# Sketched attention and an expert layer on one core: nine tiles moved into the routing, look-ahead and zero products at the start

## The chip, the core and the metric

One core of one Trainium2 chip runs the kernel. Its five engines are named here as the profile names them: PE (TensorE matmul; PEld is its weight load), DVE (VectorE), ACT (ScalarE), POOL (GpSimd) and SP (SyncE, which here only issues DMAs). Each works through its own list of instructions in order; semaphores tie the lists together. The metric is device time in microseconds (us) of one execution; lower is better.

## The reference

```python
# attention, per batch and head: r = 8, head_dim 32, 4 x 4 x 1088 positions
phi(x) = outer(S1 @ x, S2 @ x)                  # 64 numbers per position
kv, z = sum_s phi(k) v^T, sum_s phi(k)
x = phi(q) kv / (phi(q) z + 1e-6)               # N = 4352 tokens of 4 * 32 = 128 numbers
# experts: E = 8, F = 1024
logits = x @ w_gate
e = argmax(logits)                              # one expert per token
c = softmax(logits)[e] * sigmoid(x @ w_output_gate)[e]
out = c * (relu(x @ w1[e]) @ w2[e])
```

Everything is fp32. Which expert a token goes to is known only after its attention is done.

## The kernel before

The 4352 tokens are 34 chunks of 128, in nine groups of four (the last of two).

*Attention* runs as a software pipeline of steps (the loop at L456). A step may take a group of keys and a group of queries. `sketch` (L285) multiplies by S1 and S2 on PE (`ps_ab`), ACT copies half of the result out, `product` (L299) forms the outer products on DVE (`kp`, `qp`). `sums` (L332) adds keys times values into `ps_kvz` per batch; once a batch is complete, `close`, `gates_T` and `gates` make its right-hand side `kz`. A query group is transposed (`turned`, `ps_qT`), multiplied by `kz` (`attend`, `ps_nd`), and one step later divided and given its logits on DVE (`shared`, L370). The first three steps have keys alone, the last three queries alone; there are 12 steps and three more turns of the loop.

*Routing* goes by duos of groups (8, 8, 8, 4 and 6 chunks). `choose` (L391) takes the argmax and running counts per expert on DVE; in the next turn `place` (L421) turns them into positions on PE (`ps_pos`, in the PSUM buffer with the tag `rt`), and `send` (L428) makes the row numbers on DVE and lets POOL scatter the tokens' rows, one indirect DMA per chunk (L444), into a DRAM table `xs`. There each expert owns a stretch of CAP rows.

*Tables.* After the loop the counts come out of one more matmul (`ps_n`, L490), POOL scatters rows of padding behind each expert's tokens (L502), and some 20 DVE instructions (L492 to L540) make two tables for 41 tiles of 128 rows: the expert of each tile (`eti`) and its first row in `xs` (`bti`).

*Tiles.* For each tile SP reads a table entry and fetches 128 rows (`rows`, L549), and the two halves of the expert's weights (`weights`, L554, 512 KB each) into one of three buffers, unless that buffer already holds this expert; all three are filled with expert 0 at the start. On PE: `turn` (transpose, `ps_xs`), `up` (8 products, `ps_h`), then ReLU on ACT for even tiles and on DVE for odd ones, `down` (8 products, `ps_y`, which lies in the `kvz` buffer for even tiles and in `rt` for odd ones). ACT scales the result, POOL scatters it to the output (L585). A product in fp32 shows as two matmul rows in the trace. The order is written out by hand (L591 to L612): while tile t goes down, tile t+1 goes up and t+2 is turned; rows are fetched five tiles ahead, weights three.

Nothing of the tiles stands before the last of the routing, on any engine:

```python
for t in range(NX):
    rows(t)                 # reads xs: waits for every scatter, the padding's too
```

Of the kernel before, what the change touches and what calls it, by code (L numbers as in the profile page):

```python
# [12 lines left out]
F32 = mybir.dt.float32  # L13
# [6 lines left out]
GRP = 512  # L20
TS = 128
NW = 3
# [9 lines left out]
def kernel(  # L32
# [159 lines left out]
    RG = max(len(rs) for rs in routes)  # L192
    eps = consts.tile([128, 1], F32, tag="eps")
# [29 lines left out]

    KN = -(-N // TS)
    step_i = consts.tile([128, max(NT, KN)], I32, tag="step_i")
    nc.gpsimd.iota(step_i, pattern=[[1, max(NT, KN)]], base=0, channel_multiplier=0)
    step = consts.tile([128, max(NT, KN)], F32, tag="step")
    nc.gpsimd.tensor_copy(step, step_i)
    stepT = consts.tile([128, max(NT, KN)], F32, tag="stepT")
    nc.gpsimd.tensor_scalar_mul(stepT, step, float(TS))  # L230
    upto = consts.tile([128, E, E], F32, tag="upto")
    nc.gpsimd.memset(upto, 0.0)
    for e in range(E):
        nc.gpsimd.memset(upto[:, e, :e + 1], 1.0)
# [193 lines left out]
    def send(i, oh, cum, ey, pp):  # L428
# [14 lines left out]
        for j in range(n):  # L443
            apart("rows", nc.gpsimd.indirect_dma_start(  # L444
                out=xs[:, :], out_offset=bass.IndirectOffsetOnAxis(ap=sloti[:, j:j + 1], axis=0),
                in_=x[:, j], in_offset=None, bounds_check=E * CAP - 1))

    def sketches(step):  # L450
        return [None if g is None else (groups[g],) + sketch(src, groups[g]) for src, g in zip((kT, qT), step)]

    with tc.manual_schedule():
        made = sketches(steps[0])
        chosen = placed = late = None
        for n in range(len(steps) + 3):  # L456
# [3 lines left out]
            ended, fills = [], None  # L460
# [188 lines left out]
```

## Time and profile before

| | us |
|---|---|
| median of three runs | 269.72 (268.0 to 269.8) |
| the profiled execution | 269.85 |
| its span, first to last instruction | 268.1 |
| PE busy in the span | 215.1 (80%) |
| POOL busy in the span | 82.7 (31%) |
| mean granted PE clock | 0.929 of full |

The profile is one execution. Its granted clock is a share of 2.4 GHz: 1.00 is that level and 0.50 is 1.2 GHz. Busy shares are means over stages with different limits; what matters is what each stage waits for. Times in the rows below are from the span's start.

### The profile page before, as it was taken

To read this page: it belongs to the slowest core of one execution; us is meant where nothing else is said; L and a number is where in the kernel's file an instruction comes from. 1 tells how busy PE (TensorE), PEld (TensorE's weight loads), DVE (VectorE), ACT (ScalarE), POOL (GpSimd) and SP (SyncE) were. 2 spreads that over 40 slices of the span, in tenths; PEclk is the share of its full clock that TensorE was granted. 3 is DMA by queue.
4 is the path that set the end of the run, shared out by engine and by line. 5 is a ranking of instruction groups with operands and counts; after the bars stand their busy time and mean duration, and the time that the engine had idled before them with its cause. 6 is when DMAs were issued, how large, how long until landed. Compare 5 with 4: busy or idle time off the path is not lost.

```text
span 268.1 us, 6840 instructions
## 1 busy us (share of the span) xinstructions
PE 215.1 (80%) x2573; PEld 208.1 (78%) x2573; DVE 95.2 (36%) x237; ACT 58.8 (22%) x127; POOL 82.7 (31%) x135
## 2 busy tenths in 40 slices
PE   1759998999630002999999999999999999999960
PEld 1758897988530001999999999999999999999960
DVE  5134677788989000221222222222212222222200
ACT  1001423243420000122222221222222222212220
POOL 8000000575678760022212222212222122222140
PEclk9999999999965555799999999999999999999996
DMA  5999300011111112138568687887813777811000
GB/s 172 360 401 391 158 5 4 24 62 33 50 40 51 48 70 70 34 117 265 192 170 292 202 276 234 251 257 232 285 45 108 252 235 223 286 44 33 9 0 0
DMA packets 19456, 40.09 MB, mean 150 GB/s; under 512 B 3338, under 2 KB 8972, under 8 KB 19424
## 3 DMA queue, kind: packets, MB, share of 16 engines
q1 hardware_dynamic: 16880, 34.63, 39.4%
q0 software_dynamic: 2544, 5.03, 5.3%
q8 instruction: 20, 0.33, 0.5%
q14 instruction: 12, 0.10, 0.1%
HBM read 55.60 MB, written 5.48 MB: 228 GB/s over the span
## 4 chain that ended last, share of the span: by engine, by line
issue 46%; POOL 19%; DMA 2%; POOLq 2%; DVE 1%; DVEq 0%
POOL out_dram L585 14%; POOL xs L444 4%; DMA xs<-pad,pai 1%; POOLq L585 1%; DMA xin<-xs 1%; POOLq L645 0%; DVE x L379 0%; DVE L L385 0%; POOL x L441 0%; POOL x L442 0%; DVE lg L383 0%; DVE mx L400 0%; DVE sloti L435 0%; POOLq L444 0%; DVE co L440 0%
## 5 line engine op out<-in xcount | busy, mean ns | idle before, releaser
L572 PE MATMUL ps_h<-xsT,wt 128*128 128x128 f32 x656 | 81.7, 279 | 0.0
L582 PE MATMUL ps_y<-wt,hT 128*128 128x128 f32 x656 | 79.8, 275 | 0.0
L572 PEld LDWEIGHTS ps_h<-xsT,wt 128*128 128x128 f32 x656 | 78.3, 196 | 0.0
L585 POOL DMA_INDIRECT out_dram<-y,xin x41 | 39.8, 970 | 121.7 <-ACT y L584 119.0
L582 PEld LDWEIGHTS ps_y<-wt,hT 128*128 128x128 f32 x656 | 76.5, 192 | 0.0
L565 DVE COPY xsT<-ps_xs 128x128 f32<-128x128 f32 x41 | 12.0, 292 | 99.9 <-PE ps_xs L563 99.9
L444 POOL DMA_INDIRECT xs<-x,sloti x34 | 33.7, 993 | 11.2 <-issue 8.5
L576 DVE TENSOR_SCALAR hT<-ps_h 128x1024 f32<-128x1024 f32 x20 | 24.5, 1225 | 29.9 <-PE ps_h L572 29.9
L574 ACT ACTIVATE hT<-ps_h 128x1024 f32<-128x1024 f32 x21 | 21.5, 1024 | 61.6 <-PE ps_h L572 61.6
L584 ACT ACTIVATE y<-ps_y,xin 128x128 f32<-128x128 f32 x41 | 15.1, 368 | 81.3 <-PE ps_y L582 81.3
L563 PE MATMUL ps_xs<-ident,xin 128*128 128x128 f32 x41 | 11.7, 286 | 25.0 <-DMA xin<-xs 25.0
L563 PEld LDWEIGHTS ps_xs<-ident,xin 128*128 128x128 f32 x41 | 6.0, 147 | 25.3 <-DMA xin<-xs 25.3
L341 PE MATMUL ps_kvz<-vt,kp 128*64 128x65 f32 (+1 forms) x288 | 13.1, 246 | 6.3 <-DVE kp L304 6.3
L341 PEld LDWEIGHTS ps_kvz<-vt,kp 128*64 128x64 f32 (+1 forms) x288 | 11.2, 156 | 7.7 <-DVE kp L304 7.2
L304 DVE TENSOR_TENSOR kp<-ps_ab,b_sb 128x1024 f32<-128x1024 f32 (+1 forms) x9 | 10.4, 1157 | 16.3 <-ACT b_sb L296 16.3
L442 POOL TENSOR_TENSOR x<-co,ey 128x8 f32<-128x8 f32 (+2 forms) x5 | 1.4, 275 | 44.1 <-DVE co L440 44.1
L364 PE MATMUL ps_nd<-kz,qpT 128*64 128x98 f32 x272 | 13.4, 250 | 1.2 <-ACT qpT L356 1.2
L364 PEld LDWEIGHTS ps_nd<-kz,qpT 128*64 128x64 f32 x272 | 11.8, 136 | 2.3 <-ACT qpT L356 1.7
L292 PE MATMUL ps_ab<-Sb,kT 128*64 128x64 f32 x272 | 12.1, 254 | 0.5 <-DVE Sb L269 0.5
L292 PEld LDWEIGHTS ps_ab<-Sb,kT 128*64 128x64 f32 x272 | 10.9, 167 | 1.5 <-issue 0.8
L356 ACT COPY qpT<-ps_qT 128x1024 f32<-128x1024 f32 (+1 forms) x9 | 8.7, 965 | 15.4 <-PE ps_qT L354 15.4
L354 PE MATMUL ps_qT<-ident,qp 128*128 128x128 f32 x68 | 9.4, 279 | 1.9 <-DVE qp L304 1.9
(121 smaller groups left out, 123.4 us busy)
## 6 DMA issues: line engine op xcount, KB each, us to landing
wt<-in_w_dram SPq DMA_DIRECT2D x88, 512.0 KB
xin<-xs SPq DMA_DIRECT2D x41, 65.0 KB
vt<-in_v_dram SPq DMA_DIRECT2D x8, 260.0 KB
kT<-in_k_dram SPq DMA_DIRECT2D x8, 256.0 KB
qT<-in_q_dram SPq DMA_DIRECT2D x8, 256.0 KB
out_dram<-y,xin POOLq DMA_INDIRECT x41, 3.8
xs<-x,sloti POOLq DMA_INDIRECT x34, 2.3
vt<-in_v_dram SPq DMA_DIRECT2D x1, 130.0 KB
```

The costliest lines, as they stand in the source:

```text
L292: nc.tensor.matmul(ps[64 * t:64 * (t + 1), j * H:(j + 1) * H], src[:, c * 128 + 64 * t:c * 128 + 64 * (t + 1)], Sb[:, i], start=i == 0, st ...
L341: nc.tensor.matmul(acc[b][64 * h:64 * (h + 1), s], kp[p0:p0 + np_, j * H + 2 * s + h].rearrange("s i j -> s (i j)"), vt[p0:p0 + np_, c, s] ...
L364: nc.tensor.matmul(ps[64 * t:64 * (t + 1), 2 * j + s, :VG], qpT[:, 2 * j + s, 64 * t:64 * (t + 1)], kz[(c * 128 + 64 * t) // S][:, s], sta ...
L444: apart("rows", nc.gpsimd.indirect_dma_start(out=xs[:, :], out_offset=bass.IndirectOffsetOnAxis(ap=sloti[:, j:j + 1], axis=0), in_=x[:, j] ...
L563: nc.tensor.transpose(ps, xin[t][:, :DM], ident)
L565: nc.vector.tensor_copy(xTs[t], ps)
L572: nc.tensor.matmul(ps[:, c], wt[t % NW][0][:, c], xT, start=True, stop=True)
L574: nc.scalar.activation(hTs[t], ps, ACTF.Relu)
L576: nc.vector.tensor_scalar_max(hTs[t], ps, 0.0)
L582: nc.tensor.matmul(ps, hT[:, c], wt[t % NW][1][:, c], start=(c == 0), stop=(c == FC - 1))
L584: nc.scalar.activation(y, ps, ACTF.Copy, scale=x[:, DM:DM + 1])
L585: apart("out", nc.gpsimd.indirect_dma_start(out=out, out_offset=bass.IndirectOffsetOnAxis(ap=x.bitcast(I32)[:, DM + 1:DM + 2], axis=0), in ...
```

## The change

Four edits.

1. *Early tiles.* After the second duo (MARK = 1) 16 chunks have been routed. Whatever their experts, 2048 tokens fill at least NE = 9 tiles of 128 rows. `early_tiles` makes tables for these nine full tiles from the counts so far; their rows and the first weights are asked for at once, in the turn that sends the second duo. The DMA reads are declared free of the scatters of later duos (the group "early"), since those go to other rows. From the turn of the last step on, each turn of the loop also holds one tile (`tile_`), so that four tiles stand inside the loop.
2. *Late tables.* `late_tiles` makes the tables for the other 32 tiles when the last duo is sent. The tables are made with shifts, a scan and a comparison in place of the wider comparisons of before. The list of tiles starts again at expert 0 after the ninth tile.
3. *Look-ahead.* In steps without queries the next step's sketches stand on PE ahead of this step's sums.
4. *Zero products.* Ten 128x128 products of zeros (`ps_idle`) stand first on PE.

The tiles inside the loop take their ReLU from ACT alone.

```diff
+WARM = 10
-    def apart(group, ins):
+    def apart(group, ins, *others):
-        tc.declare_no_dep(ins.ins, group=group, reason="the rows are distinct")
+        for g in (group,) + others:
+            tc.declare_no_dep(ins.ins, group=g, reason="the rows are distinct")
         tc.add_to_no_dep_group(group, ins.ins)
...
+    MARK = len(duos) // 2 - 1
+    NE = -(-((routes[MARK][-1] + 1) * 128 - E * (TS - 1)) // TS)
...
+    idle = consts.tile([128, 128], F32, tag="idle")
+    nc.vector.memset(idle, 0.0)
+    ps = ps_w("ps_idle")
+    for i in range(WARM):
+        nc.tensor.matmul(ps[:, 0, :128], idle, idle, start=True, stop=True)
...
-                in_=x[:, j], in_offset=None, bounds_check=E * CAP - 1))
+                in_=x[:, j], in_offset=None, bounds_check=E * CAP - 1), *(["early"] if i > MARK else []))
...
+    def counted():
+        ps = psum.tile([128, E], F32, tag="rt", name="ps_n")
+        nc.tensor.matmul(ps, ones, state["carry"], start=True, stop=True)
+        return ps
+    def early_tiles(ps):
+        nc.vector.tensor_tensor(full, ps, ecap, op=ALU.subtract)
...
+        table(0, NE, done[:, 1:], jump, None)
+    def late_tiles(ps):
...
+        nc.gpsimd.tensor_copy(pai, pa)
+        apart("rows", nc.gpsimd.indirect_dma_start(
+            out=xs[:, :], out_offset=bass.IndirectOffsetOnAxis(ap=pai[:, :1], axis=0),
+            in_=pad.rearrange("p a b -> p (a b)"), in_offset=None), "early")
...
+        table(NE, NT - NE, ends, jump, lim[:, :1], lim[:, 1:])
...
+    def tile_(t, alone=False):
+        if t == 0:
+            turn(0)
+            turn(1)
+            up(0, alone)
+            fetch(weights, NW, 0)
+        if t + 2 < NT:
+            turn(t + 2)
+        if t + 1 < NT:
+            up(t + 1, alone)
+            fetch(weights, t + 1 + NW, 0)
+        down(t)
+        if t + NX >= NE:
+            fetch(rows, t + NX)
+        fetch(weights, t + NW, 1)
...
+            if q is None and n + 1 < len(steps):
+                made = sketches(steps[n + 1])
             if kp:
                 fills = sums(groups[k], kp, ended)
                 next(fills, None)
             if chosen:
                 placed = chosen + (place(*chosen),)
                 chosen = None
+                if placed[0] in (MARK, len(duos) - 1):
+                    ps = counted()
             qpT = turned(groups[q], qp) if qp else None
-            if n + 1 < len(steps):
+            if q is not None and n + 1 < len(steps):
                 made = sketches(steps[n + 1])
...
                 send(*placed)
+                if placed[0] == MARK:
+                    early_tiles(ps)
+                    for i in range(NE):
+                        rows(i)
+                        if i < NW:
+                            weights(i, 0)
+                            weights(i, 1)
+                elif ps:
+                    late_tiles(ps)
+                    known[0] = NT
...
+            if n >= len(steps) - 1:
+                tile_(t, True)
+                t += 1
...
+        while t < NT:
+            tile_(t)
+            t += 1
```

What stands on PE in the first steps, before (`ps_rows`: transposes of S1 and S2; `ps_ab`: sketches; `ps_kvz`: sums):

```order
L267 MATMUL ps_rows<-ident,rows_67 128x16
L267 MATMUL ps_rows<-ident,rows_68 128x16
L292 MATMUL ps_ab<-Sb,kT 64x64 x16
L341 MATMUL ps_kvz<-vt,kp 64x65 x16
L292 MATMUL ps_ab<-Sb,kT 64x64 x16
L341 MATMUL ps_kvz<-vt,kp 64x65 x16
L292 MATMUL ps_ab<-Sb,kT 64x64 x16
L341 MATMUL ps_kvz<-vt,kp 64x65 x4
```

And the same place now:

```order
L272 MATMUL ps_idle<-idle 128x128 x10
L277 MATMUL ps_rows<-ident,rows_67 128x16
L277 MATMUL ps_rows<-ident,rows_68 128x16
L302 MATMUL ps_ab<-Sb,kT 64x64 x32
L351 MATMUL ps_kvz<-vt,kp 64x65 x16
L302 MATMUL ps_ab<-Sb,kT 64x64 x16
L351 MATMUL ps_kvz<-vt,kp 64x65 x16
L302 MATMUL ps_ab<-Sb,kT 64x64 x16
L302 MATMUL ps_ab<-Sb,qT 64x64 x16
L351 MATMUL ps_kvz<-vt,kp 64x65 x20
```

Two sketches now stand ahead of the first sums, every later sketch of these steps is one place earlier, and the zero products are first.

PE where attention ends and the tiles begin, before (`ps_nd`: the last queries; `ps_pos`, `ps_n`: positions and counts of the last duo; then the tiles):

```order
L364 MATMUL ps_nd<-kz_972,qpT 64x98 x8
L424 MATMUL ps_pos<-oh,before 128x8x6
L425 MATMUL ps_pos<-cum,ones 128x8x6
L490 MATMUL ps_n<-cum,ones 128x8
L563 MATMUL ps_xs<-ident,xin 128x128 x2
L572 MATMUL ps_h<-xsT,wt_105 128x128 x8
L563 MATMUL ps_xs<-ident,xin 128x128
L572 MATMUL ps_h<-xsT,wt_107 128x128 x8
L582 MATMUL ps_y<-wt_106,hT 128x128 x8
```

And now:

```order
L374 MATMUL ps_nd<-kz_981,qpT 64x98 x8
L555 MATMUL ps_xs<-ident,xin 128x128 x2
L564 MATMUL ps_h<-xsT,wt_105 128x128 x8
L555 MATMUL ps_xs<-ident,xin 128x128
L564 MATMUL ps_h<-xsT,wt_107 128x128 x8
L574 MATMUL ps_y<-wt_106,hT 128x128 x8
L555 MATMUL ps_xs<-ident,xin 128x128
L564 MATMUL ps_h<-xsT,wt_109 128x128 x8
L574 MATMUL ps_y<-wt_108,hT 128x128 x8
L434 MATMUL ps_pos<-oh,before 128x8x6
L435 MATMUL ps_pos<-cum,ones 128x8x6
L489 MATMUL ps_n<-cum,ones 128x8
```

Two whole tiles and half of a third now stand between the last queries and the last duo's positions.

POOL from the fourth duo's rows on, before (`xs<-x,sloti`: scatters of tokens; `pad`: padding; `out_dram`: results):

```order
L441 COPY x<-ids 128x4
L442 TENSOR_TENSOR x<-co,ey 128x4
L444 DMA xs<-x,sloti 35840x130 x4
L441 COPY x<-ids 128x6
L442 TENSOR_TENSOR x<-co,ey 128x6
L444 DMA xs<-x,sloti 35840x130 x6
L502 DMA xs<-pad,pai 35840x130
L585 DMA out_dram<-y,xin 4352x128 x41
```

And now:

```order
L451 COPY x<-ids 128x4
L452 TENSOR_TENSOR x<-co,ey 128x4
L454 DMA xs<-x,sloti 35840x130 x4
L577 DMA out_dram<-y,xin 4352x128 x2
L451 COPY x<-ids 128x6
L452 TENSOR_TENSOR x<-co,ey 128x6
L454 DMA xs<-x,sloti 35840x130 x6
L513 CAST pai<-pa 128x1
L514 DMA xs<-pad,pai 35840x130
L577 DMA out_dram<-y,xin 4352x128 x39
```

The results of tiles 0 and 1 stand ahead of the last duo's scatters, and a cast ahead of the padding.

## Rows read from the trace of the kernel before

**Rows 1.** The page's first line.

```profile
span 268.1 us, 6840 instructions
```

**Rows 2.** Stages: length, busy PE, PEld, DVE, ACT, POOL, then clock, DMA share, GB/s.

```profile
6.20:20.65 14.45, 9.56 (x168) 8.98 (x168) 3.67 (x3) 0.80 (x3) 0.57 (x9) 1.00 1.03 380
62.38:75.90 13.52, 10.44 (x164) 8.72 (x160) 11.83 (x39) 5.16 (x17) 9.93 (x12) 1.00 0.14 46
75.90:104.28 28.38, 1.69 (x7) 1.44 (x7) 9.72 (x43) 0.93 (x5) 18.47 (x22) 0.51 0.18 61
104.28:110.06 5.78, 4.15 (x18) 3.86 (x19) 0.58 (x2) 0.00 (x0) 0.00 (x0) 0.50 0.11 27
110.06:259.40 149.34, 149.32 (x1336) 149.13 (x1335) 35.88 (x59) 36.21 (x61) 38.81 (x40) 1.00 0.57 181
259.40:268.10 8.70, 0.00 (x0) 0.00 (x0) 0.00 (x0) 0.37 (x1) 0.97 (x1) 0.77 0.01 0
```

**Rows 3.** Timeline, first steps: start, length, engine, line, operation, idle before it.

```profile
6.22 1.97 PE L292 MATMUL ps_ab<-Sb,kT 128*64 128x64 f32 x32 [0.51 <-DVE Sb L269]
...
9.81 2.00 PE L341 MATMUL ps_kvz<-vt,kp 128*64 128x65 f32 x32 [1.62 <-DVE kp L304]
...
20.65 1.15 PE L292 MATMUL ps_ab<-Sb,kT 128*64 128x64 f32 x32
...
25.32 1.15 PE L341 MATMUL ps_kvz<-vt,kp 128*64 128x65 f32 x32
```

**Rows 4.** Timeline, the step that routes the second duo.

```profile
58.11 0.39 PE L425 MATMUL ps_pos<-cum,ones 128*128 128x64 f32 x2
...
58.36 1.09 PE L354 MATMUL ps_qT<-ident,qp 128*128 128x128 f32 x8
...
60.33 0.22 DVE L432 TENSOR_TENSOR t<-ps_pos,oh 128x64 f32<-128x64 f32 x1
...
61.35 1.17 DVE L304 TENSOR_TENSOR qp<-ps_ab,b_sb 128x1024 f32<-128x1024 f32 x1
```

**Rows 5.** Timeline, scatters on POOL and the first tile's rows on SP.

```profile
62.38 1.03 POOL L444 DMA_INDIRECT xs<-x,sloti  x1 [0.59 <-POOL x L442]
...
73.99 1.03 POOL L444 DMA_INDIRECT xs<-x,sloti  x1 [0.59 <-POOL x L442]
...
90.84 1.01 POOL L444 DMA_INDIRECT xs<-x,sloti  x1 [0.28 <-POOL x L442]
...
98.54 0.96 POOL L502 DMA_INDIRECT xs<-pad,pai  x1 [0.30 <-issue]
102.35 0.36 SPq L552 DMA_DIRECT2D xin<-xs  x1
```

**Rows 6.** Timeline, the end of attention.

```profile
73.94 0.69 DVE L379 TENSOR_TENSOR x<-ps_nd,rc 128x512 f32<-128x512 f32 x1 [0.19 <-DMA xs<-x,sloti]
...
74.98 0.90 PE L364 MATMUL ps_nd<-kz,qpT 128*64 128x98 f32 x16 [0.67 <-ACT qpT L356]
...
76.63 0.42 DVE L379 TENSOR_TENSOR x<-ps_nd,rc 128x256 f32<-128x256 f32 x1
76.97 0.28 DVE L383 TENSOR_TENSOR lg<-ps_nd,rc 128x128 f32<-128x128 f32 x1
```

**Rows 7.** Timeline, tiles: first two up products, transposes of tiles 5 and 6.

```profile
106.65 3.62 PE L572 MATMUL ps_h<-xsT,wt 128*128 128x128 f32 x16
...
110.27 2.03 PE L572 MATMUL ps_h<-xsT,wt 128*128 128x128 f32 x16
...
121.29 0.27 PE L563 MATMUL ps_xs<-ident,xin 128*128 128x128 f32 x1
...
124.97 0.27 PE L563 MATMUL ps_xs<-ident,xin 128*128 128x128 f32 x1
```

**Rows 8.** One tile's time with heavy loads, and one without; columns as rows 2.

```profile
143.22:146.91 3.69, 3.69 (x35) 3.69 (x35) 0.29 (x1) 1.39 (x2) 0.97 (x1) 1.00 0.91 306
194.81:198.50 3.69, 3.69 (x35) 3.69 (x34) 0.29 (x1) 1.39 (x2) 0.97 (x1) 1.00 0.12 38
```

More of the change, by code (lines that the diff above doesn't have):

```diff
@@ new lines, with value, rows @@
+    regs, xin, xTs, hTs = {}, {}, {}, {}
+    def value(tab, t, top):
+        return nc.values_load(tab[0:1, t:t + 1], engines=[mybir.EngineType.SP], min_val=0, max_val=top,
+                              skip_runtime_bounds_check_because="the table is made within the bounds")
+    def rows(t):
+        at = value(bti, t, E * CAP - TS)
+        xin[t] = work.tile([TS, W], F32, tag="xin", bufs=max(NE, NX + 2), name="xin")
+        ins = nc.sync.dma_start(xin[t], xs[bass.ds(at, TS), :])
+        if t < NE:
+            tc.add_to_no_dep_group("early", ins.ins)
@@ new lines, in weights, with turn @@
+    def weights(t, a):
+        if a == 0:
+            regs[t] = value(eti, t, E - 1)
+        nc.sync.dma_start(wt[t % NW][a].rearrange("p c x -> p (c x)"),
+                          w_d[bass.ds(regs[t], 1), :, half(a)].rearrange("e p x -> p (e x)"),
+                          cond=regs[t] != (regs[t - NW] if t >= NW else 0))
+    def turn(t):
+        ps = ps_t("ps_xs")[:, :TS]
+        nc.tensor.transpose(ps, xin[t][:, :DM], ident)
+        xTs[t] = work.tile([128, TS], F32, tag="xsT", bufs=3, name="xsT")
+        nc.vector.tensor_copy(xTs[t], ps)
@@ new lines, in up, with down @@
+    def up(t, alone):
+        xT = xTs.pop(t)
+        hTs[t] = work.tile([128, FC, TS], F32, tag="hT", name="hT")
+        ps = ps_w("ps_h").rearrange("p a (c x) -> p (a c) x", x=TS)
+        for c in range(FC):
+            nc.tensor.matmul(ps[:, c], wt[t % NW][0][:, c], xT, start=True, stop=True)
+        if alone or t % 2 == 0:
+            nc.scalar.activation(hTs[t], ps, ACTF.Relu)
+        else:
+            nc.vector.tensor_scalar_max(hTs[t], ps, 0.0)
+    def down(t):
+        hT, x = hTs.pop(t), xin.pop(t)
+        ps = psum.tile([TS, DM], F32, tag=("kvz", "rt")[t % 2], name="ps_y")
+        for c in range(FC):
+            nc.tensor.matmul(ps, hT[:, c], wt[t % NW][1][:, c], start=(c == 0), stop=(c == FC - 1))
+        y = work.tile([TS, DM], F32, tag="y", bufs=4, name="y")
+        nc.scalar.activation(y, ps, ACTF.Copy, scale=x[:, DM:DM + 1])
+        apart("out", nc.gpsimd.indirect_dma_start(
+            out=out, out_offset=bass.IndirectOffsetOnAxis(ap=x.bitcast(I32)[:, DM + 1:DM + 2], axis=0),
+            in_=y, in_offset=None, bounds_check=N - 1, oob_is_err=False))
@@ L455 @@
         chosen = placed = late = None
+        t = 0
         for n in range(len(steps) + 3):
@@ L543 @@
-    regs, xin, xTs, hTs = {}, {}, {}, {}
-    def value(tab, t, top):
-        return nc.values_load(tab[0:1, t:t + 1], engines=[mybir.EngineType.SP], min_val=0, max_val=top,
-                              skip_runtime_bounds_check_because="the table is made within the bounds")
-    def rows(t):
-        at = value(bti, t, E * CAP - TS)
-        xin[t] = work.tile([TS, W], F32, tag="xin", bufs=NX + 2, name="xin")
-        nc.sync.dma_start(xin[t], xs[bass.ds(at, TS), :])
-    def weights(t, a):
-        if a == 0:
-            regs[t] = value(eti, t, E - 1)
-        nc.sync.dma_start(wt[t % NW][a].rearrange("p c x -> p (c x)"),
-                          w_d[bass.ds(regs[t], 1), :, half(a)].rearrange("e p x -> p (e x)"),
-                          cond=regs[t] != (regs[t - NW] if t >= NW else 0))
@@ L616 @@
+        waiting.sort(key=lambda w: w[0] is not rows)
+        for f, *a in waiting:
+            f(*a)
+        while t < NT:
+            tile_(t)
+            t += 1
 def kernel(**inputs):
```

167 lines of the change are left out of this document (63 added, 104 removed).

## The prediction

> **What bounds the kernel now.** I read the stage table first, then three stretches of the timeline (the first steps, the step that routes the second duo of groups, the hand-over to the tiles), then the GpSimd queue, then DMA shares of single tiles. All times count from the span's start; the profiled execution took 269.85 us with a span of 268.1 [rows 1], so 1.75 us lie around it. The median of the runs shown is 269.72 us, so nothing has to be converted.
>
> The stage table [rows 2] shows where the time is. From 110.06 to 259.40 us TensorE is busy all 149.3 us at full clock: the tiles are bound by TensorE. From 75.90 to 104.28, 28.4 us, TensorE does 1.7 us of work and GpSimd 18.5: here the kernel waits for the last scatters. From 104.28 to 110.06 the tiles begin at a granted clock of 0.50. From 6.20 to 20.65 TensorE has only 9.6 us of work in 14.4. After 259.40 comes a tail of 8.7 us that the change doesn't touch.
>
> In the hand-over the chain is GpSimd: eight scatters for the second duo from 62.38, eight for the third from 73.99, four more, six from 90.84 at (98.54 - 90.84) / 6 = 1.28 us each, the padding rows at 98.54; SP issues the first tile's rows at 102.35 [rows 5], and the first transpose starts at 104.28, where the next stage of [rows 2] begins. Attention itself ends at 74.98 + 0.90 = 75.88 [rows 6]. In steady state a tile costs 124.97 - 121.29 = 3.68 us [rows 7].
>
> **Part 1: the first steps.** Before, each early step is a chain: 32 matmul rows of the sketch (1.97 us), a ScalarE copy and the VectorE product (1.62 us with their waits, 8.19 to 9.81 [rows 3]), then 32 rows of sums; TensorE waits meanwhile. The change puts the next sketch ahead of the sums. Also the 32-row block takes 1.97 us at 6.22 and 1.15 us at 20.65 [rows 3]: a ratio of 1.71, about that of the 16 rows that took 3.62 us in the stretch at 0.50 and 2.03 us in the one at 1.00 [rows 7]. Yet the granted clock of 6.20 to 20.65 reads 1.00 [rows 2]. So I take the durations for a half clock that this row doesn't show, and the ten zero products, which run in a stretch where TensorE had nothing to do, as what lifts it. Ten fp32 products are 20 matmul rows; at half clock, 3.62 / 16 = 0.23 us each, 4.5 us. From about 1.2 us they end near 5.7, some 0.25 us after the first transposes could have begun.
>
> At full clock the new order gives: first sketch at 6.45; two sketches, 2 x 1.15, to 8.75; wait for the first product to 9.2 (copy and product again 1.6); then, without a gap, sums, sketch, sums, sketch, sketch (5 x 1.15) to 15.0; 40 rows of sums for the third step, 1.6, to 16.6; the gate transposes and their product, 1.5, to 18.1. Then come the sums that stood at 25.32 [rows 3]: 7.2 us earlier. If the clock isn't lifted before 20 us, the same sum with 1.97 for each block gives only about 2 to 4 us earlier. I take 7.2 (the durations speak for it) and keep 2 as the other end. The transfers don't hold this up: from 6.20 on they run at 380 GB/s [rows 2], so the 2.4 MB that the fourth step needs take 6.3 us even if none had come before, and it asks for them at about 12.7.
>
> The durations are all that the trace has on this. The Trainium skill, TensorE: Matmul & The Clock Gate, section Why this matters for your kernels, says that an engine that has not been working runs at the lower clock and that matmuls sent ahead warm it up. By it the sum of this part is 7.2 us; by the granted clock of 1.00 that the row gives, the zero products would be worth nothing and the part 2 to 4 us. The trace agrees in its durations and not in its clock row; no run here shows zero products.
>
> **Part 2: the step that routes the second duo.** The count for the early table is a matmul that shares a PSUM buffer with the positions, so it waits until VectorE has read these. Before, the positions were done at 58.50, the transposes of that step started in their wake at 58.36, and VectorE read the positions only at 60.33 [rows 4]. Now TensorE stands until 60.55, counts (0.4, like the second half of the positions), and the transposes start at 61.0: 2.6 us later. On VectorE eleven small instructions of the table, about 0.22 us each like the one at 60.33, stand ahead of the product at 61.35 [rows 4]: 2.5 us. The two delays lie side by side: +2.7 us for what is left of attention, so it ends at 75.88 + 2.7 = 78.6 (in times of before). The second duo's scatters are ahead of this on GpSimd and don't move.
>
> **Part 3: when the tiles begin.** Rows of the first nine tiles need the first two duos' scatters alone; before, VectorE was let go by the last of these at 73.94 [rows 6]. With 1.9 us for the read (102.35 to 104.28) tile 0 is on chip at 75.9, and tile 1 behind it, before TensorE is free at 78.6. So tiles begin at 78.6 instead of 104.28: 25.7 us earlier.
>
> Until the transpose of tile 5 before needed 121.29 - 104.28 = 17.0 us, including the half clock and waits for rows. Now: two transposes and the first up product 2.7; the second transpose's copy and three VectorE steps of the last group (0.42 and 0.28 [rows 6] and a reciprocal) that free the PSUM buffer for the next up product, 1.6; up and down 3.9; tile 1, 3.7; the last positions and the count, which wait for ScalarE and VectorE, 1.9; tile 2, 3.7: 17.5 us, so the transpose of tile 5 stands at 96.1. That is 25.2 us earlier, if the clock stays up. Attention's last products leave TensorE gaps below a microsecond, and before it only read 0.51 once the engine had stopped [rows 2].
>
> **Part 4: when the late tiles can follow.** Tile 9 is asked for four tiles on, at 96.1 + 4 x 3.68 = 110.8. On GpSimd the third duo's scatters now start with part 2's delay, at 76.7; from there to the padding is 98.54 - 73.99 = 24.55 us as before [rows 5], plus two output scatters put ahead of the last duo's (2 x 1.28, as for the others) and a cast, about 0.3 with its wait: padding at 104.1. Landed and read as before (3.8 and 1.9 us [rows 5]): 109.9. That is 0.9 us ahead of need. But weights and output are now in flight, so the landing may take 1 to 2 us more; I add 0.6 us. SP is a queue: the load of the second half of tile 7's weights stands behind the read of tile 9, but is needed only at 113. The outputs of tiles 2 to 8 stand behind the padding on GpSimd; four result buffers carry that until tile 6, whose copy waits about 1 us on ScalarE without reaching TensorE.
>
> **Part 5: weights.** A tile loads weights only if its buffer holds another expert. With the reference's inputs the experts have 547, 583, 461, 483, 494, 867, 420 and 497 tokens, of which 307, 185, 191, 208, 280, 409, 232 and 236 are in the first 16 chunks. The tile list then loads 21 times before and 30 times after: 9.4 MB more. Tiles 2 to 26 load all but once. Such a tile moves 1.05 MB of weights and 0.13 MB of rows and results; in 3.68 us that is 320 GB/s. Before, one tile with heavy loads ran at 306 GB/s at a share of 0.91, one without at 0.12 [rows 8]: full share is about 336 GB/s. So it fits with some 5% to spare, and each load is issued three tiles (11 us) ahead: I cost it at nothing. Without that cover 290 GB/s would cost 0.4 us a tile, less some 9 us of lead: about 1 us.
>
> **Sum.** 269.85 - 7.2 - 25.2 + 0.6 = 238.0 us.
>
> **Rivals.**
> *A, the start stays slow.* Granted clock 1.00 from the start [rows 2] speaks for it, the two durations of one block [rows 3] against it. Then part 1 gives 3 us: 242.2. Chance 0.13.
> *B, the late rows come late.* GpSimd carries the chain and has only 0.9 us to spare; a scatter that takes 1.5 us under load instead of 1.28 adds 0.22 x 21 = 4.6 us, 3.7 of them seen by TensorE: 241. Against it: the eight scatters from 62.38 with the small operations behind them took 11.6 us, 1.28 x 9, beside a VectorE busy 11.8 us of 13.5 [rows 2, 5]. Chance 0.14.
> *C, weights starve the tiles, and the kernel is slower.* Place: tiles 2 to 26, whose loads never pause now. It decides when 25 x (1.18 MB / rate - 3.68 us) - 9 exceeds the 32 us won, so below 221 GB/s. At 210 it is 25 x 1.94 - 9 = 39 us: 277. For it: 30 loads instead of 21, and a backlog of scatters on the same engines. Against it: 306 GB/s were measured [rows 8]. Chance 0.03, a third of it within 1%.
> *D, the early reads wait for all scatters after all.* Then only part 1 remains, 269.85 - 7.2 = 262.6. The early reads stand ahead of the third duo's scatters in the program, so nothing can make them wait. Chance 0.01.
>
> **How the numbers follow.** The forecast keeps 0.69. Its own range is 235 (half a microsecond off the attention delay, no wait at tile 9, first steps 1 us better) to 241. A and B reach to 242 and, with the worse ends (2 us at the start, 5 us at tile 9), to 246: range 234.5 to 246. Faster by over 1%, which is about what a measurement of this kernel tells from no change: 0.69 + 0.13 + 0.14 + 0.01 = 0.97; within 1%: 0.01; slower by over 1%: 0.02.
>
> **What would show it.** Right: the 32-row sketch block at the start takes about 1.15 us; the first tile transpose stands near 71.4 (78.6 - 7.2), TensorE at 1.00 from there to the end, hardly idle before tile 9; the first tile's read is let go by the eighth scatter of the second duo; DMA share near 0.95 in tiles 9 to 26 without TensorE waiting for weights. Wrong: a block of 1.97 us at the start (A), a gap in TensorE before the transpose of tile 9 (B), products that wait for weights (C), or no tile before the last scatter (D).

## The result, and the profile after

| | before | after |
|---|---|---|
| median, us (five runs each) | 269.72 (268.0 to 269.8) | 246.38 (242.6 to 246.5) |
| ratio, 95% interval | | 0.908 (0.899 to 0.917) |
| the profiled execution | 269.85 | 242.6 |
| its span | 268.1 | 240.9 |
| mean granted PE clock | 0.929 | 0.977 |

The change makes the kernel 9% faster. The ratio goes by the two executions of after that the record counts as fast, 242.6 and 246.17 us with their middle at 244.4; the other three, 246.4 to 246.5, lie within 0.4 us of the second. The forecast was 238.0 us with a range of 234.5 to 246.0: 244.4 lies inside, and so does the profiled execution, 4.6 us above the forecast; the median of all five lies 0.4 us above the range's end. The profile is of the fastest of the five, by 3.6 us.

The page of after, its first lines (span; busy time and share of each engine):

```profile
span 240.9 us, 6878 instructions
PE 216.8 (90%) x2595; PEld 208.6 (87%) x2595; DVE 92.4 (38%) x246; ACT 60.9 (25%) x129; POOL 81.8 (34%) x127
```

Stages of after (length, busy PE, PEld, DVE, ACT, POOL, clock, DMA share, GB/s), which answer to [rows 2] and [rows 8]:

```profile
6.14:18.24 12.10, 9.92 (x271) 9.05 (x271) 6.21 (x7) 1.70 (x6) 0.26 (x1) 0.99 1.04 378
18.24:21.76 3.52, 3.52 (x42) 3.23 (x41) 0.00 (x0) 0.21 (x1) 0.00 (x0) 0.56 1.05 373
55.16:58.63 3.47, 3.47 (x42) 3.02 (x42) 2.40 (x14) 1.01 (x1) 1.84 (x3) 0.55 0.06 19
73.92:90.81 16.89, 14.71 (x125) 13.93 (x124) 7.96 (x41) 5.76 (x11) 13.03 (x17) 1.00 0.86 257
90.81:112.39 21.58, 19.31 (x167) 18.52 (x165) 5.05 (x12) 5.28 (x9) 11.94 (x13) 1.00 0.83 285
112.39:232.10 119.71, 119.71 (x1071) 119.56 (x1071) 28.64 (x47) 28.17 (x48) 32.02 (x33) 1.00 0.69 231
112.39:119.76 7.37, 7.37 (x66) 7.37 (x67) 1.81 (x3) 1.39 (x2) 1.94 (x2) 1.00 1.00 364
```

The 28.4 us in which TensorE waited for scatters [rows 2] are gone: the tiles follow attention at once, and from 112.39 on TensorE doesn't wait. The last row shows two tiles with heavy weight traffic, a DMA share of 1.00, and TensorE busy throughout. What is new are the second and third rows: stretches in which TensorE has work, at about half clock.

TensorE in the first steps and in the step of the second duo, which answer to [rows 3, 4]:

```profile
1.17 3.98 PE L272 MATMUL ps_idle<-idle 128*128 128x128 f32 x20 [1.17 <-DVE idle L269]
6.14 2.08 PE L302 MATMUL ps_ab<-Sb,kT 128*64 128x64 f32 x64 [0.55 <-DVE Sb L279]
...
18.24 2.00 PE L351 MATMUL ps_kvz<-vt,kp 128*64 128x65 f32 x32
20.17 1.66 PE L364 MATMUL ps_qT<-ident,qp 128*128 128x128 f32 x8
...
52.45 0.39 PE L435 MATMUL ps_pos<-cum,ones 128*128 128x64 f32 x2
54.91 0.39 PE L489 MATMUL ps_n<-cum,ones 128*128 128x8 f32 x2 [2.08 <-DVE t L442]
55.16 1.64 PE L364 MATMUL ps_qT<-ident,qp 128*128 128x128 f32 x8
56.72 1.98 PE L302 MATMUL ps_ab<-Sb,qT 128*64 128x64 f32 x32
```

Two sketches now take 2.08 us together, so one takes about half of the 1.97 us of before. The sums at 18.24 stood at 25.32 [rows 3], 7.1 us later; but they take 2.00 us where the same 32 matmul rows took 1.15. The count (`ps_n`) waits 2.08 us for VectorE, as forecast, and the 40 rows behind it run at about half clock.

The hand-over to the late tiles, on TensorE, GpSimd and SP, which answers to [rows 5, 7]:

```profile
90.81 0.27 PE L555 MATMUL ps_xs<-ident,xin 128*128 128x128 f32 x1
92.21 2.05 PE L564 MATMUL ps_h<-xsT,wt 128*128 128x128 f32 x16 [1.12 <-DVE xsT L557]
...
107.35 0.33 PE L555 MATMUL ps_xs<-ident,xin 128*128 128x128 f32 x1 [0.26 <-DMA xin<-xs]
107.52 1.96 PE L564 MATMUL ps_h<-xsT,wt 128*128 128x128 f32 x16
109.89 2.02 PE L574 MATMUL ps_y<-wt,hT 128*128 128x128 f32 x16 [0.42 <-DMA wt<-in_w_dram]
112.39 0.33 PE L555 MATMUL ps_xs<-ident,xin 128*128 128x128 f32 x1 [0.48 <-DMA xin<-xs]
```

```profile
98.75 0.98 POOL L514 DMA_INDIRECT xs<-pad,pai  x1 [0.28 <-DMA wt<-in_w_dram]
```

```profile
94.29 4.01 SPq L549 DMA_DIRECT2D wt<-in_w_dram  x3
105.29 0.33 SPq L542 DMA_DIRECT2D xin<-xs  x1
```

The transpose of tile 5 is at 90.81, that of tile 9 at 107.35, of tile 10 at 112.39. Padding issued at 98.75 lets the read go at 105.29, 6.5 us later; before it was 3.8 [rows 5]. SP's waits ahead of reads (us in total, times, longest):

```profile
SPq L542 <- DMA xs<-x,sloti: 9.2, 1, 9.2
SPq L542 <- DMA xs<-pad,pai: 6.4, 1, 6.4
```

One wait for a token scatter, then one for the padding: the early reads don't wait for later scatters.

### The profile page after: what moved, and what is told of

Its sections match the earlier page's. It is cut to its first block, busy times and chain, and to the rows that moved or that the text cites. A ratio compares the mean times of both kernels' runs of the same rounds, so it can differ in the third digit from the quotient of the medians.

```text
span 240.9 us, 6878 instructions
## 1 busy us (share of the span) xinstructions
PE 216.8 (90%) x2595; PEld 208.6 (87%) x2595; DVE 92.4 (38%) x246; ACT 60.9 (25%) x129; POOL 81.8 (34%) x127
## 4 chain that ended last, share of the span: by engine, by line
PE 27%; issue 23%; POOL 8%; DMA 4%; DVE 3%; POOLq 1%; ACT 1%; SPq 0%; DVEq 0%
PE ps_h L564 14%; PE ps_y L574 12%; POOL out_dram L577 8%; DMA wt<-in_w_dram 3%; DMA xin<-xs 2%; PE ps_xs L555 1%; POOLq L577 1%; POOLq L705 0%; ACT hT L566 0%; DVE x L389 0%; DVE L L395 0%; DVE sloti L445 0%; DVE past L473 0%; PE ps_pos L434 0%; DVE eti L472 0%
## 5 line engine op out<-in xcount | busy, mean ns | idle before, releaser
L564 PE MATMUL ps_h<-xsT,wt 128*128 128x128 f32 x656 | 80.3, 275 | 2.5 <-DVE xsT L557 1.5
L564 PEld LDWEIGHTS ps_h<-xsT,wt 128*128 128x128 f32 x656 | 76.5, 192 | 3.3 <-DVE xsT L557 2.0
L566 ACT ACTIVATE hT<-ps_h 128x1024 f32<-128x1024 f32 x23 | 23.6, 1024 | 40.0 <-PE ps_h L564 40.0
L568 DVE TENSOR_SCALAR hT<-ps_h 128x1024 f32<-128x1024 f32 x18 | 22.0, 1225 | 27.0 <-PE ps_h L564 27.0
L351 PE MATMUL ps_kvz<-vt,kp 128*64 128x65 f32 (+1 forms) x288 | 12.2, 235 | 2.7 <-DVE kp L314 2.2
L351 PEld LDWEIGHTS ps_kvz<-vt,kp 128*64 128x64 f32 (+1 forms) x288 | 10.5, 146 | 3.8 <-DVE kp L314 2.7
L366 ACT COPY qpT<-ps_qT 128x1024 f32<-128x1024 f32 (+1 forms) x9 | 8.7, 965 | 19.8 <-PE ps_qT L364 19.8
L364 PE MATMUL ps_qT<-ident,qp 128*128 128x128 f32 x68 | 10.5, 302 | 1.9 <-DVE qp L314 1.9
L302 PE MATMUL ps_ab<-Sb,qT 128*64 128x64 f32 x272 | 10.7, 234 | 0.5 <-issue 0.5
L314 DVE TENSOR_TENSOR qp<-ps_ab,b_sb 128x1024 f32<-128x1024 f32 (+1 forms) x9 | 10.4, 1152 | 1.0 <-ACT b_sb L306 1.0
L302 PEld LDWEIGHTS ps_ab<-Sb,qT 128*64 128x64 f32 x272 | 9.7, 148 | 1.2 <-issue 1.2
```

The lines of the kernel that those rows point to most:

```text
L302: nc.tensor.matmul(ps[64 * t:64 * (t + 1), j * H:(j + 1) * H], src[:, c * 128 + 64 * t:c * 128 + 64 * (t + 1)], Sb[:, i], start=i == 0, st ...
L314: nc.vector.tensor_mul(res[:, :n], bview(av, [list(av.ap[1]), list(av.ap[2]), [0, r]]), bview(bv, [list(bv.ap[1]), [0, r], list(bv.ap[2])]))
L351: nc.tensor.matmul(acc[b][64 * h:64 * (h + 1), s], kp[p0:p0 + np_, j * H + 2 * s + h].rearrange("s i j -> s (i j)"), vt[p0:p0 + np_, c, s] ...
L564: nc.tensor.matmul(ps[:, c], wt[t % NW][0][:, c], xT, start=True, stop=True)
L566: nc.scalar.activation(hTs[t], ps, ACTF.Relu)
L568: nc.vector.tensor_scalar_max(hTs[t], ps, 0.0)
```

## Experiments

The runs fell on two sorts of chips. On one sort the kernel before takes 269.7 us, as above; on the other 284.4 to 285.6. Each ratio is to the kernel before on the same chip, and times of runs are set side by side only within a sort. On the second sort:

**The change itself again.** No edit.

> The changed kernel itself once more, for a second profile of it. The first profile stands at 242.6 us and shows two stretches at a granted clock of 0.50 inside attention, 18 to 21.7 and 55.2 to 58.5 us, each behind a wait of TensorE; the median of its executions is 246.4. Theory 1 (how often the clock falls behind such waits differs from execution to execution): times spread between 242 and 247, and a profile of 246 shows one or two more stretches at 0.50. Theory 2 (the spread comes from the transfers): the same stretches at 0.50, but longer waits for rows or weights.

268.06 us (267.0 to 269.0) against 285.63: ratio 0.938 (0.933 to 0.943), a gain of 17.6 us and not 23.3. The spread of 242 to 247 that the run was to explain can't be judged at these times. The sums of the fourth step stand at 18.42 and take 1.15 us: the clock fall at 18 us in the profile of after doesn't come in every execution. The fall behind the count comes here too, and lasts longer (stage as above, clock 0.50):

```profile
62.00:68.00 6.00, 5.59 (x54) 4.76 (x56) 3.02 (x17) 1.01 (x1) 3.20 (x4) 0.50 0.07 22
```

Much of what makes this chip slower shows on TensorE, and in the same stretches on VectorE and ScalarE, as idle time that nothing in the profile ends ("issue"). A piece of it:

```profile
47.20 0.34 PE L351 MATMUL ps_kvz<-vt,kp 128*64 128x65 f32 x4 [0.38 <-issue]
48.66 0.49 PE L351 MATMUL ps_kvz<-vt,kp 128*64 128x65 f32 x3 [1.13 <-issue]
49.39 0.37 PE L364 MATMUL ps_qT<-ident,qp 128*128 128x128 f32 x1 [0.24 <-issue]
50.11 0.68 PE L364 MATMUL ps_qT<-ident,qp 128*128 128x128 f32 x2 [0.35 <-issue]
```

From 46.4 to 54.4 a few rows come every 0.7 or 1.4 us, while GpSimd scatters at its usual 1.28 us. There are four such stretches (from about 46, 69, 90 and 119), each some microseconds behind the first scatter of a duo (42.8, 64.2, 87.2, 111.2). The profiles on the first sort of chip have none.

**No zero products.**

```diff
-    for i in range(WARM):
-        nc.tensor.matmul(ps[:, 0, :128], idle, idle, start=True, stop=True)
```

> The change without the ten zero products; look-ahead stays. Theory 1 (the zero products lift the clock from the start): 32 sketch rows at 6 us take about 2.0 us again instead of 1.1, sums of the fourth step start near 20 to 23 instead of 18.2 us, the time rises by 2 to 4 us. Rival (the look-ahead alone does it): blocks of 1.1 us from the start and the same time within 1 us.

273.5 us, ratio 0.954 (0.946 to 0.961; the change: 0.938): 5.4 us slower by the medians, more than the 2 to 4 expected. First two sketches and sums of the fourth step:

```profile
6.34 3.68 PE L299 MATMUL ps_ab<-Sb,kT 128*64 128x64 f32 x64 [0.79 <-DVE Sb L276]
...
21.26 2.00 PE L348 MATMUL ps_kvz<-vt,kp 128*64 128x65 f32 x32
```

3.68 us for what took 2.08, and the fourth step's sums 2.8 us later, themselves at 2.00; the sketch behind them is 4.5 us later (24.99 against 20.53). For the first sketches the zero products do what part 1 took them to do, and up to 17.4 us the run is 1.7 us behind. The other 2.8 us come behind that, where the clock fell as it did in the profile of after with the zero products. Whether leaving them out had a part in that fall isn't shown.

**No look-ahead.**

```diff
-            if q is None and n + 1 < len(steps):
-                made = sketches(steps[n + 1])
...
-            if q is not None and n + 1 < len(steps):
+            if n + 1 < len(steps):
```

> The change with the sketches of the first steps back behind the sums; zero products stay. Theory 1 (look-ahead takes the waits of TensorE out of the first steps): waits of 1.6 us before each of the first products' sums return, the fourth step's sums start near 22 instead of 18.2 us, plus 4 us in all, and if the clock falls in these waits up to 2 more: 246 to 249 against 242.6. Rival (the zero products alone win the start): within 1 us of the change.

269.69 to 274.22 us in four executions, where the change took 267.0 to 269.0. There is no interval: by the two shorter executions the loss is 3 us, by all four 5 us, and the trace has to carry it. The waits of 1.62 us for the product are back, and the fourth step's sums stand at 22.94, 4.5 us later.

**The start alone, on the kernel before.** Zero products and look-ahead put into the kernel before.

> The kernel before with two of the four edits alone: zero products and look-ahead; tiles and tables as before. Theory 1 (the first steps are worth about 6 to 7 us, and all that follows hangs on TensorE and GpSimd behind them, so the gain reaches the end): faster than before by 5 to 7.5 us. Rival (the hand-over to the tiles swallows it, since it waits for the scatters): under 2 us. The rest of the change's gain would then be the early tiles'.

280.0 us against 285.44, ratio 0.980 (0.972 to 0.988): 5.4 us that reach the end, though in this profile the first two sketches take 3.66 us in spite of the zero products. That leaves the other 12 us of the 17.6 to the early tiles and what goes with them, by subtraction: they weren't run alone. In this kernel TensorE meets stretches of slow issue at 47 to 55 and 68 to 77; in the change two more fall into the early tiles, where TensorE now has work. That fits a gain that is smaller here than on the first sort, and isn't shown beyond that.

**Products of zeros in the wait for the count.**

```diff
+                    if placed[0] == MARK:
+                        keep = ps_w("ps_keep")
+                        for i in range(8):
+                            nc.tensor.matmul(keep[:, 0, :128], idle, idle, start=True, stop=True)
                     ps = counted()
```

> The change with eight zero products (16 matmul rows, some 1.95 us) put into the wait of TensorE between the positions of the second duo and its count. Theory 1 (the clock falls because TensorE stands there for 2.1 us): the granted clock stays at 1.00 from 55 to 59 us, the eight transposes take 1.1 instead of 1.64 and the sketch 1.15 instead of 1.98, attention ends 1.2 us earlier and so does the kernel, if tile 9's rows are not what then decides. Rival (the clock's level there has nothing to do with this wait): no change, or a gain that returns as a wait for tile 9's rows.

269.26 us, ratio 0.943 (0.940 to 0.947), no gain on the change's 0.938. The place itself:

```profile
59.96 2.00 PE L636 MATMUL ps_keep<-idle 128*128 128x128 f32 x16
62.21 0.39 PE L489 MATMUL ps_n<-cum,ones 128*128 128x8 f32 x2 [0.25 <-DVE t L442]
62.46 1.07 PE L364 MATMUL ps_qT<-ident,qp 128*128 128x128 f32 x8
63.46 1.15 PE L302 MATMUL ps_ab<-Sb,qT 128*64 128x64 f32 x32
```

With TensorE kept at work, the same wait for VectorE costs no clock: 1.07 and 1.15 us where the change took 1.95 and 1.98, and the next products 2.3 us earlier (64.88 against 67.21). This alone doesn't show that the wait brings the clock down, since the same wait can leave it up, as in the run without the zero products at the start:

```profile
67.21 0.39 PE L486 MATMUL ps_n<-cum,ones 128*128 128x8 f32 x2 [2.08 <-DVE t L439]
67.46 1.07 PE L361 MATMUL ps_qT<-ident,qp 128*128 128x128 f32 x8
```

Seven profiles have a wait of 1.8 to 2.1 us there. The granted clock behind it was 0.50 to 0.55 in four of them (the change twice, no look-ahead, and the late table alone below) and 1.00 in three (no zero products, no weights, and the shorter path below). In the four profiles in which the wait is filled or gone, the transposes and the sketch took 1.07 to 1.09 and 1.15 us each time. So the clock fell at this place only where the wait stood, and not in every profile that has it. What decides isn't shown, and with so few profiles chance isn't excluded. The next stretch of slow issue took the gain back; the first tile's transpose stands at 88.82 and 89.05.

**No weights for the tiles.**

```diff
-        nc.sync.dma_start(wt[t % NW][a].rearrange("p c x -> p (c x)"),
-        ...
+        pass
```

> The change without any load of weights for tiles: all tiles multiply by the weights of expert 0 that are loaded at the start, so the values are not the reference's. Theory 1 (weights share the DMA engines with the scatters and with the late rows, which makes the padding land after 6.5 us instead of 3.8 and tiles 9 and 10 wait): no wait for rows or weights at tiles 8 to 10, the padding lands within 4 us, the kernel 1.5 to 3 us faster than the change on such a chip. Rival (tile 9 waits for GpSimd's queue alone, weights cost nothing): the padding lands as late, within 1 us of the change.

265.67 us, ratio 0.929 (0.921 to 0.936): 2.4 us under the change by the medians, at the edge of what these runs tell. Without weights SP waits for the padding: issued at 119.05, it lets the read go at 122.86, after 3.8 us. That is the value of [rows 5], where no tile's weights are in flight either; with them it was 6.5 us in the profile of after. This fits theory 1: the traffic of the weights makes the padding land late. But the change's own profile on this sort of chip (119.06 to 125.44) can't be set beside it. There SP has no wait for the padding; the read stands behind weight loads on SP's own list, and goes out right behind them (104.53 + 20.33 = 124.86):

```profile
104.53 20.33 SPq L549 DMA_DIRECT2D wt<-in_w_dram  x9
125.44 0.33 SPq L542 DMA_DIRECT2D xin<-xs  x1
```

And TensorE waits for no rows there: from 127.17 a tile follows every 3.68 us. So the 2.4 us aren't shown to come from the landing.

**A shorter path for the late rows.** Three edits: results of the first tiles behind the padding on GpSimd, the late table's VectorE work behind a tile's copy, and weights ahead of rows on SP:

```diff
+        fetch(weights, t + NW, 1)
         if t + NX >= NE:
             fetch(rows, t + NX)
-        fetch(weights, t + NW, 1)
```

> The change with the way to the late tiles shortened: the results of tiles 0 to 2 are scattered behind the padding instead of ahead of the last duo's scatters (eight result buffers, twelve of rows), the late table stands on VectorE behind the transpose's copy of that turn, and the second half of the weights is asked for ahead of the late rows. Theory 1 (tiles 4 and 8 to 10 lose 1.1 + 1.4 us in the change to the late table and the late rows): about 2 to 2.5 us faster than the change on such a chip, no wait of TensorE between tile 4 and tile 12. Rival (these waits only take the place of others): within 1 us of the change.

272.21 us, ratio 0.955 (0.950 to 0.961): 4 us slower than the change, against both theories. The read goes out only at 130.88, but it isn't the padding, issued at 120.54, that holds it. Again SP has no wait for the padding; the read stands behind weight loads, one of which the third edit put ahead of it (105.86 + 24.50 = 130.36):

```profile
105.86 24.50 SPq L556 DMA_DIRECT2D wt<-in_w_dram  x10
130.88 0.33 SPq L549 DMA_DIRECT2D xin<-xs  x1
```

Nor is the late read what costs the time. TensorE waits for no rows and no weights between tiles 4 and 12, as theory 1 said; transposes of tiles 6 to 9 and the slow issue between the first two:

```profile
118.42 0.27 PE L562 MATMUL ps_xs<-ident,xin 128*128 128x128 f32 x1
...
125.33 0.80 PE L581 MATMUL ps_y<-wt,hT 128*128 128x128 f32 x2 [0.56 <-issue]
...
129.79 0.42 PE L562 MATMUL ps_xs<-ident,xin 128*128 128x128 f32 x1
...
134.33 0.27 PE L562 MATMUL ps_xs<-ident,xin 128*128 128x128 f32 x1
...
138.01 0.27 PE L562 MATMUL ps_xs<-ident,xin 128*128 128x128 f32 x1
```

In the change, on this sort of chip, they stand at 118.31, 127.17, 130.86 and 134.54. The 3.4 us by which this profile is longer come between 118 and 134, from slow issue that lasts longer and a slow product behind it (16 rows in 2.70 us). Whether the edits have a part in that isn't shown. With the zero products in the wait added:

> The shortened way to the late tiles together with the eight zero products ahead of the second duo's count. Theory 1: both gains add up, since with the late rows earlier nothing holds back the 1.2 to 2 us that a clock at 1.00 wins in attention: 3 to 4.5 us faster than the change on such a chip. Rival (the zero products only move a wait, as they did beside the change): no faster than the shortened way alone.

272.9 us, ratio 0.954, no better. The next run takes one of the three edits alone.

On the first sort of chip (before 269.72 us):

**The late table alone.**

```diff
+        return num
+    def late_table(num):
         left = consts.tile([128, E], I32, tag="left")
...
                 tile_(t, True)
                 t += 1
+            if rest:
+                late_table(num)
+                known[0] = NT
```

> Only one of the three edits of the late-path run: the late table's VectorE instructions stand behind the copy of the tile turned in that turn; results, weights and buffers stay as in the change. Theory 1 (the copy's wait is worth its 1.1 us only if TensorE, not the padding, sets when tile 9 begins; the 4 us that the late-path run lost came from its other two edits): the wait of about 1.1 us for the tile's copy ahead of that tile's up product goes, and the kernel takes 0 to 1 us less than the change (ratio to before 0.934 to 0.938). Rival (the late table is on the path of the late rows, so putting it back was what cost the late-path run its 4 us): tile 9's rows are asked for 1 to 4 us later than in the change and the ratio is 0.945 to 0.955.

243.11 us (241.67 to 244.98), ratio 0.905 (0.898 to 0.912): at or below the change's 0.908, and no loss (the ratios expected were those of the other sort of chip). Weights and first late read on SP, and the padding:

```profile
92.76 4.01 SPq L552 DMA_DIRECT2D wt<-in_w_dram  x3
103.31 0.33 SPq L545 DMA_DIRECT2D xin<-xs  x1
```

```profile
98.85 0.98 POOL L514 DMA_INDIRECT xs<-pad,pai  x1 [0.28 <-DMA wt<-in_w_dram]
```

The wait of 1.12 us for the copy is gone, so the tile's weights are issued 1.5 us earlier than in the change (92.76 against 94.29); and the read is let go 2.0 us earlier (103.31 against 105.29), though the padding is issued at the same time (98.85 and 98.75).

**The count later.**

```diff
-                if placed[0] in (MARK, len(duos) - 1):
+                if placed[0] == len(duos) - 1:
                     ps = counted()
...
-                    early_tiles(ps)
+                    early_tiles(counted())
```

> The count for the early tables stands behind that step's transposes and sketches on TensorE, when VectorE has read the positions, instead of ahead of them; everything else as in the change. Theory 1 (TensorE's wait of 2.0 to 2.1 us for the read of the positions, and the clock of 0.50 behind it, are what part 2 costs): the transposes follow the positions at once, at 1.00, and the last queries' step ends 2 to 3 us earlier; ratio to before 0.928 to 0.932. Rival (the eleven small VectorE instructions of the table ahead of the next product hold the step anyway): the product starts about 1.1 us earlier in place of 3, TensorE waits for it instead, and the kernel is within 1 us of the change (0.934 to 0.940).

243.73 us, ratio 0.902 (0.893 to 0.911); the intervals tell it neither from the late table's nor from the change's. The step, and the end of attention:

```profile
52.85 1.09 PE L364 MATMUL ps_qT<-ident,qp 128*128 128x128 f32 x8
53.88 1.15 PE L302 MATMUL ps_ab<-Sb,qT 128*64 128x64 f32 x32
...
59.95 1.09 PE L364 MATMUL ps_qT<-ident,qp 128*128 128x128 f32 x8 [1.54 <-DVE qp L314]
...
71.86 1.45 PE L374 MATMUL ps_nd<-kz,qpT 128*64 128x98 f32 x16 [0.67 <-ACT qpT L366]
```

No wait ahead of the transposes, and no half clock there; but 1.54 us of waiting for the product come instead, as the rival said. The step ends 1.2 us earlier than in the change, and part of that is lost where the clock falls at 71.9 (1.45 us for 16 rows that took 0.90). Here the padding is issued 1.05 us earlier than in the change (97.70), and its landing lets the read go at 105.56, no earlier: 11.0 us after the last three weight loads ahead of it began to be issued (94.58), as in the change (94.29 to 105.29) and, within half a microsecond, with the late table alone (10.6). From the padding it is 7.9, 6.5 and 4.5 us. So in these three profiles, where SP does wait for the padding, the read follows the weights and not the padding's issue.

**The kernel before, once more.**

> The kernel before, for its own profile on such a chip. Theory 1 (what makes the chip slower are stretches of 5 to 8 us in which TensorE, VectorE and ScalarE issue an instruction only every 0.7 to 1.4 us, one behind the scatters of each duo): two such stretches lie inside attention, as with the start edits alone, the later ones where TensorE waits for the scatters anyway, and the time is about 285 us; tiles in the stretch bound by TensorE take 3.68 us as on the first chip. Rival (the chip is slower throughout, by 6%): no such stretches, and a tile takes 3.9 us.

268.79 us: it fell on the first sort of chip and shows no slow issue at all, so it tells neither theory apart. Its first steps differ from those of [rows 3]: without any zero products, 32 rows of sums take 1.15 us from 15.04 on, and the fourth step's sums stand at 23.79 and not at 25.32. So the kernel before, too, differs there from one execution to the next, by 1.5 us.

**Both: count and late table later** (on the second sort of chip).

> Both edits of the last two timed runs: the count for the early tables behind that step's transposes and sketches, and the late table's VectorE instructions behind the copy of the tile turned in that turn. Theory 1 (the two act at different places: the first frees 1.2 to 1.6 us of TensorE in the step of the second duo; the second lets the weights of the next tile be issued 1.5 us earlier, behind which the padding lands, so that the rows of tile 9 come about 2 us earlier): no wait of 2.1 us ahead of the count, no wait of 1.1 us and more for the copy ahead of that tile's up product, the read of tile 9 let go about 10.6 us after the weights issued ahead of it, near 102.5, and a ratio to before of 0.890 to 0.898. Rival (what the first frees is lost again where attention ends, at a clock of 0.50 behind a wait of 1.5 us for the next product): the first tile's transpose stands where it stood, near 73 to 74, and the ratio is 0.900 to 0.908, that of the late table alone.

264.49 us (263.39 to 266.26) against 284.37, ratio 0.934 (0.929 to 0.939). The change's on such a chip was 0.938 (0.933 to 0.943): lower, but the intervals overlap (the ratios expected were those of the first sort). The two waits are gone and the first tile's transpose is at 85.43 (the change: 89.05), and slow issue lies over the same stretches. The read goes out at 123.30, 7.8 us after the padding and 7.2 after the last three weight loads ahead of it began to be issued, and not the 10.6 expected: that figure doesn't carry over to this sort of chip. TensorE waits for no rows here either. Whether the two gains add up on the first sort of chip wasn't tried.

## Why the forecast was right, and where it was too low

*What bounds the kernel.* Right: the wait for scatters was there to be won, and it was won.

That the time lies in the range is in part luck: the range reached to 246 for the sake of rivals A and B, and what filled it was the clock and the landing, by other ways than theirs.

*Part 1, first steps: 7.2 us.* The working holds to 18.24: 7.1 us earlier than in the profile of before, 5.6 earlier than in its second one. On the second sort of chip, taking the zero products away costs 5.4 us and taking the look-ahead away 3 to 5, and both together gain 5.4 on the kernel before: as far as these sums go, each needs the other. The step that failed is one that the sum didn't name: that the clock, once lifted, stays up. Between 14.5 and 18.2 TensorE waits twice, 0.55 us for VectorE and 0.46 for ScalarE; the clock fell, and the next 40 rows took 3.66 us and not 2.24. Cost in the profile: 1.4 us. The waits alone don't explain it: all ten profiles with both start edits have them, and the clock fell in three. Rival A is out in this execution: without the zero products two blocks take 3.68 us and with them 2.08, though the granted clock reads 1.00 either way, as it did in [rows 2]. Its sign came in three other profiles, where the blocks took 3.66 to 3.68 us with the zero products; its price didn't, since the fourth step's sums still stood at 19.4 to 19.8, 5.5 to 6 us earlier than in [rows 3] and not 3.

The Trainium skill, TensorE: Matmul & The Clock Gate, section Why this matters for your kernels, has an idle engine at the lower clock and matmuls sent ahead as the cure. The run without zero products agrees for the first sketches (3.68 us against 2.08); the three profiles just named, with 3.66 to 3.68 us behind the same products, do not.

*Part 2: +2.7 us.* The wait was 2.08 us as costed. Behind it the transposes and sketches took 1.64 and 1.98 us, and not 1.09 and 1.15: 1.4 us more. The part priced the wait and not the clock that can fall behind it. Where the prediction does speak of that, in part 3, it took from a clock of 0.51 "once the engine had stopped" [rows 2] that only long stops matter; that reading is the step that failed: behind waits of 1.8 to 2.1 us the clock fell in four of seven profiles. That it fell in this one is chance as far as the runs show. Attention ends at 73.99; 75.88 - 7.2 + 2.7 = 71.4 was forecast.

*Part 3: tiles begin 25.7 us earlier.* Right, but for what parts 1 and 2 left over: with part 1's gain the first transpose was forecast at 71.4 and stands at 73.92. From the first tile transpose to that of tile 5 it took 16.9 us; 17.5 was forecast.

*Part 4: +0.6 us for the late rows.* Mis-sized: from the transpose of tile 5 to that of tile 10 it took 21.58 us, where five tiles of 3.68 us and the 0.6 make 19.0: 2.6 us more. One part wasn't in the sum: the late table's VectorE work stands ahead of a tile's copy, 1.12 us on TensorE. The other is Rival B's effect by another mechanism. It had GpSimd's scatters slowed to 1.5 us each; they kept to 1.28 and the padding was issued at 98.75 (104.1 - 7.2 = 96.9 forecast; the third duo's scatters began 2.6 us late, at 72.09). What was late was the landing, 6.5 us and not the 3.8 to 5.8 that I allowed, beside weights that are in flight. The run without weights gives 3.8 again (on the other sort of chip), and the late table alone, which moves weights and not padding, moves the read by 2.0 us.

*Part 5: weights at nothing.* Right for the tiles, where TensorE is busy throughout at 364 GB/s; the 336 GB/s that I took for full share was too low. Rival C is out. Its sign came once: a product waited 0.42 us for weights, at 109.89, whose load stands behind the late read on SP; the forecast had that load in time. So the weights are not free. With the landing of the padding the way from the transpose of tile 8 to that of tile 11 took 12.9 us and not 11.0, some 2 us more. Rival D is out by SP's two waits.

*Sum.* 1.4 (clock, first steps) + 1.2 (clock behind the count: attention ends 2.6 late, of which 1.4 are the first) - 0.6 (tiles 0 to 4) + 2.6 (late hand-over) = 4.6 us, which is what the profile has.

*The median* is another 3.8 us above the profiled execution; the one of 246.17 us shows a mean granted clock of 0.968 and the profiled one 0.977. Half clock loses half its time: (1 - 0.977) x 240.9 = 5.5 us against (1 - 0.968) x 243.9 = 7.8 us, an estimate of 2.3 of the 3.0 us between their spans. But an execution with a mean clock of 0.959 has a span of 244.0, by the same estimate 2.2 us more than that of 243.9, so the mean clock doesn't settle it. Where the clock fell in the others isn't recorded, and the cause of these 3.8 us stays open. The first steps differ between profiles, too: with zero products ahead, the first two sketches took 2.08 or 2.09 us in seven of them and 3.66 to 3.68 in three. The range left no room for a clock that differs from one execution to the next.

*What stays open.* Why some chips issue slowly after scatters begin; what makes the clock fall behind the same wait in one execution and not in another; why the late-path run is slower, since TensorE didn't wait for its late read; what the early tiles give alone; and whether both later edits add up.

## What to carry over

A new wait on TensorE costs its own length and may cost the clock as well: here, behind some 2 us, the 40 rows that followed took 1.4 to 1.7 us more in four of seven profiles. Forecast both cases, or fill the wait. A small transfer that others wait for can land late beside bulk transfers: in three profiles here its landing kept pace with the weight loads, not with its own issue. But look first at the queue that issues the read: on the second sort of chip the read stood behind loads on SP's own list, and TensorE didn't wait for it at all. And the gain was 23.3 us on one sort of chip and 17.6 on the other, so measure on a second chip before a gain is carried forward.

## What the runs showed of the hardware that I had not expected

- Behind two waits of about 0.5 us the granted clock was 0.54 to 0.56 over the next 3.5 to 3.6 us in three of ten profiles, and behind the same waits the same rows took 2.1 us in the other seven.
- Behind a wait of 1.8 to 2.1 us it was 0.50 to 0.55 in four of seven profiles and 1.00 in three.
- The granted clock reads 1.00 over the first sketches without zero products, which take 1.8 times as long as with them.
- On chips where the kernel takes 6% longer, TensorE, VectorE and ScalarE issue only every 0.7 to 1.4 us for 5 to 8 us after a duo's scatters begin, with or without weight traffic, while GpSimd keeps its pace.
